# A fused attention and feed-forward kernel: TensorE kept in written order while the position bias is made, and one pair's operand splits moved from GpSimd to ScalarE and VectorE

## The chip, the cores and the metric

The kernel runs on one core of a Trainium2 chip. The metric is device time in microseconds (us) of one execution. One execution was also profiled; times inside it are counted from the start of its span. Engines are named as in the profile: PE is TensorE, with its weight loads as PEld; DVE is VectorE; ACT is ScalarE; POOL is GpSimd; SP only issues transfers. An "issue" row of SP (SPq) is the time that SP needs to hand a transfer over, not the transfer itself.

## The reference, cut to what matters

```python
scores = scale * np.matmul(q, k.transpose(0, 1, 3, 2))      # 4 batches, 8 heads, 576 x 576, head size 64
x = (np.log1p(abs(pos_i - pos_j)) / np.log1p(max(pos_i, 1)))[..., None]
bias = np.maximum(x @ w1 + b1, 0.0) @ w2                    # hidden size 32, one bias plane for each head
attn = softmax(scores + bias)                               # over the last axis
x = heads_side_by_side(attn @ v)                            # 4 x 576 x 512
u = x + np.real(fft(fft(x, axis=1), axis=2))
un = (u - mean(u)) / np.sqrt(var(u) + 1e-06)
out = u + np.maximum(un @ w_ch1, 0.0) @ w_ch2               # 512 -> 2048 -> 512
```

## The kernel before

The work falls into three stages.

**The bias stage** (some 80 us) makes the bias planes. It runs over 144 steps, four to a group `u` (36 groups). For each step one tile of hidden values is made: three of every four on VectorE (`hd`, L334, 108 in all) and one on ScalarE (`ha`, L332, 36). Two small matmuls of TensorE (L353) then reduce it into a PSUM tile `bps` of the group; there are three such tiles. ScalarE evacuates each group into one of four quarters of `ring` (L302, 36 evacuations), and after every fourth group SP sends that quarter out: to the `bias` tiles of head pair 0 in SBUF (L311, for the last groups `bias_r` in L218 to L221) and to DRAM (`bias_d`, L314). VectorE has eight buffers for `hd`, ScalarE six for `ha`.

**Attention** runs over 16 units, a unit being a pair of heads and a batch. A unit's q and k arrive by four transfers into `qT` and `kT` (one buffer each, so the next unit's loads wait until these are read). `prep` turns them into a rounded high part and a low rest, in eight splits: `qs` and `kh` by `hi` (L181), the low halves of `qs` and `kl` by `lo` (L184), all on GpSimd. There are two buffers of each. `scores` are four matmuls to a tile (L243), `largest` adds the bias and finds the row maximum on VectorE (L261, here called the maximum step), `expo` is the exponential on ScalarE (L269). Nine score tiles make a unit. Those of unit 0 are computed inside the bias stage already, by `first_scores`: tiles 0 to 5 in pairs at the steps that the list `due` names (a number WAIT after the step at which their bias rows begin a block), 6, 7 and 8 after its last step. During the bias stage there is one PSUM buffer for a score tile. Then come the turns, one for each unit; a turn's steps are written out in `ORDER`, and TensorE, VectorE and ScalarE keep that order. The steps `W0` to `W3` make one chunk of a weight matrix 32-bit: a transfer into `raw` (L138), one ScalarE instruction (L140, `wf`) and three of VectorE (L141 to L143). The first chunk's `raw` shares its buffer with `sm`, the small tables of the bias stage, so its transfer waits until that stage is over.

**The feed-forward stage** follows: the Fourier sums, the normalization and two matrix products.

What orders instructions: the compiler layer lists each engine's instructions by a simulated timeline, except on engines that a `manual_schedule` block keeps in written order. Before the change only the turns have such a block. Each engine then works through its own list in order and waits at an instruction whose inputs or buffers are not ready.

Of the kernel before, what the change touches and what calls it, by code (L numbers as in the profile page):

```python
# [9 lines left out]
F32 = mybir.dt.float32  # L10
# [3 lines left out]
AF = mybir.ActivationFunctionType  # L14
ALU = mybir.AluOpType
# [10 lines left out]
ND = 258  # L26
NF = FF // P
FCN = 15
L0, L1 = 0, 42
WAIT = 20  # L30
EV = 40
AHEAD = 19
HB = {"d": 8, "a": 6}
# [14 lines left out]
ORDER = """  # L48
# [61 lines left out]
def body(ctx, tc, a, out):  # L110
    nc = tc.nc
# [46 lines left out]
    def load(n):  # L158
        hp, b = units[n]
        t = []  # L160
        for nm, w in (("qT", 2 * S), ("kT", KW)):
            f = ldp.tile([P, w], F32, tag=nm, name=nm)
            for e in range(2):
                nc.sync.dma_start(f[64 * e:64 * e + 64], a[nm][hp, b])
            t.append(f)
        ld[n] = t

    def load_v(n):
        hp, b = units[n]
        v = vt[n] = vp.tile([P, 5, P], F32, tag="v", name="v")  # L170
        nc.sync.dma_start(v, a["v"][hp, b].rearrange("(t p) c -> p t c", p=P))

    def prep(n):
        q, k = ld.pop(n)
        qs = stp.tile([P, 2 * S], F32R, tag="qs", name="qs")
        kh = stp.tile([P, KW], F32R, tag="kh", name="kh")
        kl = stp.tile([P, KW], F32R, tag="kl", name="kl")
        stk[n] = (qs, kh, kl)

        def hi(dst, src, c):  # L180
            nc.gpsimd.tensor_scalar(dst[:, c], src[:, c], 1.0, 0.0, ALU.mult, ALU.add)  # L181

        def lo(dst, src, ref, rows, c):
            nc.gpsimd.tensor_tensor(dst[rows, c], src[rows, c], ref[rows, c].bitcast(F32), ALU.subtract)  # L184

        every, low = slice(0, 128), slice(64, 128)
        ca, cb, ck = slice(0, S), slice(S, 2 * S), slice(S, KW)
        return [
            lambda: hi(qs, q, ca), lambda: lo(qs, q, qs, low, ca),
            lambda: hi(kh, k, ca), lambda: lo(kl, k, kh, every, ca),  # L190
            lambda: hi(qs, q, cb), lambda: lo(qs, q, qs, low, cb),
            lambda: hi(kh, k, ck), lambda: lo(kl, k, kh, every, ck),
        ]
# [72 lines left out]
    def expo(n, i):  # L266
        blk = (BLK if n else BLK0)[i]
        p = prob(n, blk)
        nc.scalar.activation(  # L269
            p, p, AF.Exp, bias=nms[n][:, blk:blk + 1], scale=-1.0, accum_out=sums[n][:, blk:blk + 1])  # L270

    def first_scores(i):
        scores(0, i)
        largest(0, i)
        expo(0, i)

    with ExitStack() as st:
        hpool = pool("hp", 1, stack=st)
        ring = xp.tile([P, 4, 4, S], F32, tag="x", name="ring")
        bps = pool("bps", 3, PSUM, stack=st)  # L280
        sps = pool("sps0", 1, PSUM, stack=st)

        sm = rawp.tile([P, 66 + 5 * NG], F32, tag="raw", name="sm")
        w1c, b1c, w2 = sm[:, 0:1], sm[:, 1:2], sm[:, 2:66].rearrange("p (r c) -> p r c", r=2)
        lt, inv = sm[:, 66:66 + 4 * NG], sm[:, 66 + 4 * NG:]
        nc.sync.dma_start(sm, a["sm"])
        parts = ((512, 1148), (0, 512), (1148, NT0 + S))
        for i, (c0, c1) in enumerate(parts):
            (nc.sync if i else nc.scalar).dma_start(tw[:, c0:c1], a["tab"][:, c0:c1])
        nc.vector.tensor_scalar(lt, lt, b1c, None, ALU.mult)  # L290
        for i, (c0, c1) in enumerate(parts):
            if i == 9:
                nc.scalar.activation(tw[:, c0:c1], tw[:, c0:c1], AF.Copy, scale=w1c)
            else:
                nc.vector.tensor_scalar(tw[:, c0:c1], tw[:, c0:c1], w1c, None, ALU.mult)

        def bias_evac(u, ps):
            g = u % 4
            o = ring[:, u // 4 % 4]
            dst = o[:, g].rearrange("p (c s) -> p c s", c=2)  # L300
            if u % EV != EV - 1:
                nc.scalar.activation(dst, ps[:, :, :CH], AF.Copy, scale=inv[:, u:u + 1])  # L302
            else:
                nc.vector.tensor_scalar(dst, ps[:, :, :CH], inv[:, u:u + 1], None, ALU.mult)
            if g < 3:
                return
            r0 = 16 * (u - 3)
            src = o.rearrange("(r h) g s -> r h g s", h=H)
            for e in range(2):
                if r0 < 512:  # L310
                    nc.sync.dma_start(bt[0, r0 // 128][r0 % 128:r0 % 128 + 64, e], src[:, e])  # L311
                else:
                    rest_bias(bt[0, 4], e, src[:, e])
            nc.sync.dma_start(bias_d[4 * (u - 3):4 * (u + 1)].rearrange("r h g s -> (r h) g s"), o)  # L314
            if u % 8 == 7:
                due.extend([(4 * u + WAIT, u // 8 * 2), (4 * u + WAIT + 2, u // 8 * 2 + 1)])

        pending, early = [], []
        due = []
        ps = None  # L320
        steps = bias_steps()
        ahead = {}

        def hidden(n):
            u, t4, _, low, _ = steps[n]
            col = lt[:, 4 * u + t4:4 * u + t4 + 1]
            off = NT0 if low is None else N0 - low
            src = tw[:, off:off + S]
            who = WHO[n % len(WHO)]
            h = hpool.tile([P, S], F32, tag="h" + who, name="h" + who, bufs=HB[who])  # L330
            if who == "a":
                nc.scalar.activation(h, src, AF.Relu, bias=col)  # L332
            else:
                nc.vector.tensor_scalar(h, src, col, 0.0, ALU.add, ALU.max)  # L334
            return h

        for n, (u, t4, rev, low, _) in enumerate(steps):
            for k in range(n, min(n + AHEAD, len(steps))):
                if k not in ahead and (k <= n + 2 or WHO[k % len(WHO)] != "d"):
                    ahead[k] = hidden(k)  # L340
            if n in (L0, L1):
                load(n // L1)
                load_v(n // L1)
                early.extend(prep(n // L1))
            if early and n % 2:
                early.pop(0)()
            while due and due[0][0] <= n:
                first_scores(due.pop(0)[1])
            h = ahead[n]
            if t4 == 0:  # L350
                ps = bps.tile([P, 2, 512], F32, tag="ps", name="bps")
            for c in range(2):
                nc.tensor.matmul(  # L353
                    ps[32 * t4:32 * t4 + 32, c, :CH], w2[:, int(rev)], h[:, c * CH:(c + 1) * CH],
                    start=True, stop=True, tile_position=(0, 32 * t4),
                )
            if t4 == 3:
                pending.append((u, ps))
            if t4 == 2 and len(pending) > 1:
                bias_evac(*pending.pop(0))  # L360
        for e in pending:
            bias_evac(*e)
        for i in [i for _, i in due] + [8]:
            first_scores(i)


    x = xp.tile([P, B, 5, DM], F32, tag="x", name="x")
    with mid, ExitStack() as st:
# [112 lines left out]
        def first_column():  # L481
# [20 lines left out]
            engines={mybir.EngineType.PE, mybir.EngineType.DVE, mybir.EngineType.Activation}))  # L502
        for n in range(U + 4):
            pr = prep(n + 1) if 1 < n + 1 < U else []
            wd = []
            if n < NF:
                wf = rawp.tile([P, 512], F32, tag="wf", name="wf")
                wd = widen(a["m1"][:, P * n:P * n + P].rearrange("(k p) c -> p k c", p=P), wf, [P, 4, P], rawp)
            for i, w in enumerate(ORDER):
                w, u = w.rstrip("'"), n - w.count("'")  # L510
                if w[0] == "W":
                    if u < NF:
                        wd[int(w[1])]()
                elif 0 <= u < U and (u or w[0] not in "SDX"):
                    steps[w[0]](u, w)
                if i % 8 == 4 and pr:
                    pr.pop(0)()
            assert not pr
            if n < NF:
                nc.sync.dma_start(w1_d[n].rearrange("p k c -> p (k c)"), wf)  # L520
            if n + 2 < U:
                load(n + 2)
            if n == 6:
                fs = tabp.tile([P, 3, 2, 2, NK], F32R, tag="tab", name="fs")
                nc.gpsimd.tensor_copy(fs[0:1, 0, 0, 0, 0:1], vt[6][0:1, 0, 0:1])
                nc.gpsimd.dma_start(fs, a["fs"])
            if n == FCN:
                first_column()


    with ExitStack() as st:
# [201 lines left out]
        for b in range(B):  # L733
# [4 lines left out]
            if b + 1 < B:  # L738
                tl, un, pcs = prepare(b + 1)
                n = 4  # L740
            else:
                un, pcs = norm(rest_tiles)
                n = 2
# [67 lines left out]
```

## Time and profile before

| | |
|---|---|
| time, median of 3 runs | 814.06 us (811.08, 814.06 and one far longer, 4077.4) |
| time of the profiled execution | 811.41 us |
| its span, first to last instruction | 809.6 us |
| mean granted clock of TensorE, of full speed | 0.971 |
| PE busy | 762.1 us, 94% |
| DVE busy | 430.8 us, 53% |
| ACT busy | 432.1 us, 53% |
| POOL busy | 378.3 us, 47% |

The shares are means over stages that have different limits. The bias stage lies at 4 to 78 us of the span, the first turns run until about 100, the steady turns until about 320.

### The profile page before, as it was taken

To read this page: it belongs to the slowest core of one execution; us is meant where nothing else is said; L and a number is where in the kernel's file an instruction comes from. 1 tells how busy PE (TensorE), PEld (TensorE's weight loads), DVE (VectorE), ACT (ScalarE), POOL (GpSimd) and SP (SyncE) were. 2 spreads that over 40 slices of the span, in tenths; PEclk is the share of its full clock that TensorE was granted. 3 is DMA by queue.
4 is the path that set the end of the run, shared out by engine and by line. 5 is a ranking of instruction groups with operands and counts; after the bars stand their busy time and mean duration, and the time that the engine had idled before them with its cause. 6 is when DMAs were issued, how large, how long until landed. Compare 5 with 4: busy or idle time off the path is not lost. (4 is left out here: it accounts for less than half of the span.)

```text
span 809.6 us, 13075 instructions
## 1 busy us (share of the span) xinstructions
PE 762.1 (94%) x4786; PEld 619.8 (77%) x4786; DVE 430.8 (53%) x935; ACT 432.1 (53%) x875; POOL 378.3 (47%) x317
## 2 busy tenths in 40 slices
PE   3997799999999999957998999999999999999997
PEld 2454688878887888637886888888888887888896
DVE  5796666666666666889598351531417322111311
ACT  5696587787878787634433342333333333332453
POOL 5602364566446640032555534544346444444695
PEclk8899799999999999987999999999999999999999
DMA  6888568778747631174423221111210112111332
GB/s 158 249 261 303 151 170 261 211 182 250 199 119 206 189 96 41 66 259 157 140 95 117 92 91 39 40 53 51 80 53 27 55 49 91 53 45 47 118 91 66
DMA packets 55376, 101.63 MB, mean 126 GB/s; under 512 B 7568, under 2 KB 26128, under 8 KB 53904
## 3 DMA queue, kind: packets, MB, share of 16 engines
q1 hardware_dynamic: 54880, 97.44, 40.6%
q0 software_dynamic: 288, 3.02, 1.2%
q8 instruction: 38, 0.62, 0.3%
q10 hardware_dynamic: 144, 0.33, 0.1%
q14 instruction: 26, 0.21, 0.1%
HBM read 74.38 MB, written 23.72 MB: 121 GB/s over the span
## 5 line engine op out<-in xcount | busy, mean ns | idle before, releaser
L691 DVE SCALAR_TENSOR_TENSOR hl<-hp,hh 128x512 fp32r<-128x512 f32 (+1 forms) x80 | 50.7, 634 | 222.0 <-ACT hh L690 222.0
L663 POOL TENSOR_TENSOR w2l<-w2f,w2h 128x512 fp32r<-128x512 f32 x80 | 104.1, 1302 | 113.4 <-ACT w2h L662 108.4
L663 POOL TENSOR_TENSOR w1l<-w,w1h 128x512 fp32r<-128x512 f32 x80 | 108.2, 1353 | 93.4 <-ACT w1h L662 89.9
L261 DVE CUSTOM_DVE_ANT_0 p<-s,bias 128x576 f32<-128x576 f32 x128 | 95.5, 755 | 77.9 <-PE s L243 74.4
L685 PE MATMUL hp<-ul,w1h 128*128 128x512 f32 (+1 forms) x320 | 118.1, 369 | 1.4 <-DVE ul L655 1.4
L685 PE MATMUL hp<-uh,w1l 128*128 128x512 f32 (+1 forms) x320 | 118.0, 369 | 0.0
L685 PE MATMUL hp<-uh,w1h 128*128 128x512 f32 (+1 forms) x320 | 118.0, 369 | 0.0
L243 PE MATMUL s<-kh,qs 128*128 128x288 f32 (+1 forms) x320 | 101.2, 335 | 13.5 <-DVE nm L261 6.8
L699 PE MATMUL acc<-w2h,hh 128*128 128x512 f32 x288 | 112.2, 391 | 0.0
L699 PE MATMUL acc<-w2l,hh 128*128 128x512 f32 x288 | 112.0, 390 | 0.0
L662 ACT ACTIVATE w2h<-w2f 128x512 fp32r<-128x512 f32 x80 | 50.5, 632 | 114.6 <-POOL w1l L663 61.2
L381 ACT ACTIVATE pt<-t 128x512 f32<-128x512 f32 x144 | 82.5, 595 | 51.6 <-PE t L401 35.6
L699 PE MATMUL acc<-w2h,hl 128*128 128x512 f32 x288 | 105.3, 395 | 2.9 <-DVE hl L691 2.9
L662 ACT ACTIVATE w1h<-w 128x512 fp32r<-128x512 f32 x80 | 50.3, 630 | 105.0 <-PE hp L685 96.8
L269 ACT ACTIVATE p<-p,nm 128x576 f32<-128x576 f32 x128 | 98.0, 773 | 1.2 <-DVE nm L261 1.2
L181 POOL TENSOR_SCALAR kh<-kT 128x576 fp32r<-128x576 f32 (+1 forms) x32 | 28.8, 916 | 138.3 <-PE s L243 95.9
L243 PE MATMUL s<-kl,qs 128*128 128x288 f32 (+1 forms) x320 | 89.8, 298 | 0.0
L422 PE MATMUL o<-pt,v 128*64 128x288 f32 x640 | 86.7, 417 | 0.0
L243 PEld LDWEIGHTS s<-kh,qs 128*128 128x128 f32 (+1 forms) x320 | 59.3, 185 | 30.7 <-POOL kh L181 7.2
L401 PE MATMUL t<-ident,p 128*128 128x128 f32 x576 | 79.8, 275 | 0.3 <-ACT pt L381 0.3
L685 PEld LDWEIGHTS hp<-ul,w1h 128*128 128x128 f32 x320 | 60.4, 189 | 12.0 <-DVE ul L655 1.7
L401 PEld LDWEIGHTS t<-ident,p 128*128 128x128 f32 x576 | 68.4, 141 | 1.1 <-ACT pt L381 0.7
(125 smaller groups left out, 1377.4 us busy)
## 6 DMA issues: line engine op xcount, KB each, us to landing
raw<-m SPq DMA_DIRECT2D x32, 512.0 KB, 3.9
w2f<-w_d SPq DMA_DIRECT2D x64, 256.0 KB, 2.6
bias_d<-ring SPq DMA_DIRECT2D x9, 1152.0 KB, 6.1
kT<-kT SPq DMA_DIRECT2D x32, 304.0 KB, 5.0
qT<-qT SPq DMA_DIRECT2D x32, 288.0 KB, 4.5
bias<-bias_d SPq DMA_DIRECT2D x24, 288.0 KB, 5.0
v<-v SPq DMA_DIRECT2D x16, 320.0 KB, 3.2
out<-x SPq DMA_DIRECT2D x18, 256.0 KB, 2.7
```

What stands on the lines that cost most here:

```text
L181: nc.gpsimd.tensor_scalar(dst[:, c], src[:, c], 1.0, 0.0, ALU.mult, ALU.add)
L243: nc.tensor.matmul(ps[:m, c, :CH], qs[:, c0:c0 + m], kk[:, k0 + c * CH:k0 + (c + 1) * CH], start=k == 0, stop=k == 1, skip_group_check=True)
L261: nc.vector.tensor_tensor_reduce(p, bank.pop((n, i))[:, :, :CH], bias, -0.125, 3.0e38, ALU.add, ALU.min, nms[n][:, blk:blk + 1])
L269: nc.scalar.activation(p, p, AF.Exp, bias=nms[n][:, blk:blk + 1], scale=-1.0, accum_out=sums[n][:, blk:blk + 1])
L381: nc.scalar.activation(dst, src, AF.Copy)
L401: nc.tensor.transpose(tp[:, 128 * t:128 * t + 128], pb[t].rearrange("p h s -> p (h s)")[:, k0:k0 + 128], ident)
L422: nc.tensor.matmul(os_[u][e, c, :CH], vt[u][:, j, e], pts[u][:, 2 * j + h if j < 4 else 8, c * CH:(c + 1) * CH], start=j == 0, stop=j == 4 ...
L662: nc.scalar.activation(h, src, AF.Copy)
L663: nc.gpsimd.tensor_tensor(l, src, h.bitcast(F32), ALU.subtract)
L685: nc.tensor.matmul(ps[:, :N], (wh, wl)[wi][:, P * kb:P * kb + P], ut[ui][:, kb, :N], start=i == 0, stop=i == len(mm) - 1)
L691: nc.vector.scalar_tensor_tensor(hl[:, :N], ps[:, :N], 0.0, hh[:, :N].bitcast(F32), ALU.max, ALU.subtract)
L699: nc.tensor.matmul(acc[t], h[i][:, P * t:P * t + P], w[j], start=f == 0 and k == 0, stop=f == NF - 1 and k == 2)
```

## The change

In the bias stage TensorE is put in written order. With it the loads and the splits of unit 0 are written ahead of the loop. WAIT goes from 20 to 24. The eight splits of unit 1 are taken out of the loop and off GpSimd: `hi` becomes a copying ACTIVATE of ScalarE, `lo` a TENSOR_TENSOR of VectorE, and they are written between the score tiles 7 and 8 of unit 0, in a block in which TensorE, VectorE and ScalarE all keep the written order. In turn 0, `ORDER` is sorted so that the `W` steps come last.

```diff
-L0, L1 = 0, 42
-WAIT = 20
+L1 = 42
+WAIT = 24
...
         def hi(dst, src, c):
-            nc.gpsimd.tensor_scalar(dst[:, c], src[:, c], 1.0, 0.0, ALU.mult, ALU.add)
+            if n == 1:
+                nc.scalar.activation(dst[:, c], src[:, c], AF.Copy)
+            else:
+                nc.gpsimd.tensor_scalar(dst[:, c], src[:, c], 1.0, 0.0, ALU.mult, ALU.add)
 
         def lo(dst, src, ref, rows, c):
-            nc.gpsimd.tensor_tensor(dst[rows, c], src[rows, c], ref[rows, c].bitcast(F32), ALU.subtract)
+            eng = nc.vector if n == 1 else nc.gpsimd
+            eng.tensor_tensor(dst[rows, c], src[rows, c], ref[rows, c].bitcast(F32), ALU.subtract)
...
-        pending, early = [], []
+        pending = []
...
+        fixed = ExitStack()
+        fixed.enter_context(tc.manual_schedule(engines={mybir.EngineType.PE}))
+        load(0)
+        load_v(0)
+        early = prep(0)
         for n, (u, t4, rev, low, _) in enumerate(steps):
...
-            if n in (L0, L1):
-                load(n // L1)
-                load_v(n // L1)
-                early.extend(prep(n // L1))
+            if n == L1:
+                load(1)
+                load_v(1)
...
-        for i in [i for _, i in due] + [8]:
+        fixed.close()
+        fixed.enter_context(tc.manual_schedule(engines={
+            mybir.EngineType.PE, mybir.EngineType.DVE, mybir.EngineType.Activation}))
+        for _, i in due:
             first_scores(i)
+        for piece in prep(1):
+            piece()
+        first_scores(8)
+        fixed.close()
...
-            for i, w in enumerate(ORDER):
+            for i, w in enumerate(ORDER if n else sorted(ORDER, key=lambda w: w[0] == "W")):
```

**Where the first score tile stands on PE.** TensorE's list near the start of the bias stage; `bps` rows are the bias matmuls, `s` rows those of a score tile. Before:

```order
L353 MATMUL bps<-ha,sm 32x288 x2
L353 MATMUL bps<-hd,sm 32x288 x4
L243 MATMUL s<-kh,qs 128x288
L353 MATMUL bps<-hd,sm 32x288 x2
L353 MATMUL bps<-ha,sm 32x288 x2
L353 MATMUL bps<-hd,sm 32x288 x6
L353 MATMUL bps<-ha,sm 32x288 x2
L243 MATMUL s<-kl,qs 128x288
L243 MATMUL s<-kh,qs 128x288
L243 MATMUL s<-kl,qs 128x288
```

TensorE's list now, at the place of its first score tile:

```order
L361 MATMUL bps<-ha,sm 32x288 x2
L247 MATMUL s<-kh,qs 128x288
L247 MATMUL s<-kl,qs 128x288
L247 MATMUL s<-kh,qs 128x288
L247 MATMUL s<-kl,qs 128x288
L361 MATMUL bps<-hd,sm 32x288 x4
L247 MATMUL s<-kh,qs 128x288
L247 MATMUL s<-kl,qs 128x288
L247 MATMUL s<-kh,qs 128x288
L247 MATMUL s<-kl,qs 128x288
```

The first matmul on unit 0's splits stood after 18 steps (four groups and two steps); it now stands after 52 (13 groups), and the second tile of the pair only two steps behind the first.

**The first pair on DVE.** VectorE's list from there; the rows `p,nm` and `nm` are a maximum step. Before:

```order
L334 TENSOR_SCALAR hd<-tw,sm 128x576 x36
L261 ISA p,nm<-s,bias 128x576
L261 ISA nm 128x1
L334 TENSOR_SCALAR hd<-tw,sm 128x576 x8
L261 ISA p,nm<-s,bias 128x576
```

VectorE's list now, at the same place:

```order
L338 TENSOR_SCALAR hd<-tw,sm 128x576 x39
L265 ISA p,nm<-s,bias 128x576
L265 ISA nm 128x1
L338 TENSOR_SCALAR hd<-tw,sm 128x576 x2
L265 ISA p,nm<-s,bias 128x576
```

The first maximum step stands behind 47 hidden tiles (2, 6 and 39) where it stood behind 44, and two tiles part it from the second, where eight did. The later pairs move likewise.

**The end of the bias stage.** ScalarE's list; `p,sm` rows are exponentials, `ring` rows evacuations. Before:

```order
L302 ACTIVATE ring<-bps,sm 128x576 x2
L269 ACTIVATE p,sm<-p,nm 128x576
L302 ACTIVATE ring<-bps,sm 128x576 x5
L269 ACTIVATE p,sm<-p,nm 128x576 x2
L269 ACTIVATE pr,sm<-pr,nm 128x576
L140 ACTIVATE wf<-raw 128x512
```

ScalarE's list now, at the end of the stage:

```order
L306 ACTIVATE ring<-bps,sm 128x576 x5
L273 ACTIVATE p,sm<-p,nm 128x576
L306 ACTIVATE ring<-bps,sm 128x576
L273 ACTIVATE p,sm<-p,nm 128x576
L182 ACTIVATE qs<-qT 128x576
L182 ACTIVATE kh<-kT 128x576
L182 ACTIVATE qs<-qT 128x576
L182 ACTIVATE kh<-kT 128x640
L273 ACTIVATE pr,sm<-pr,nm 128x576
L140 ACTIVATE wf<-raw 128x512
```

The four `hi` splits stand ahead of tile 8's exponential, and the last evacuation (group 35) now stands behind tile 6's exponential. On VectorE the four `lo` splits stand likewise between the maximum steps of tiles 7 and 8. On SP, the four loads of unit 2, which stood among the bias transfers, now stand right behind the transfer of the first `raw`. No row of the first weight chunk (L140 to L143) has moved against its neighbours.

## Rows read from the trace of the kernel before

**Rows 1.** Windows: from:to, length, busy time (instructions) of each engine, PEclk, DMA share, GB/s.

```profile
13.50:20.00 6.50, 0.09 (x2) 0.00 (x0) 1.98 (x5) 1.45 (x3) 6.33 (x5) 0.69 0.05 12
39.80:72.00 32.20, 32.13 (x378) 19.06 (x372) 31.68 (x77) 30.66 (x53) 0.00 (x0) 1.00 0.83 271
100.00:120.00 20.00, 20.00 (x160) 16.00 (x157) 11.60 (x35) 17.11 (x41) 13.10 (x12) 1.00 0.60 168
```

**Rows 2.** Timeline of PE: start, length, engine, line, operation [idle before it <-what ended that].

```profile
20.30 0.61 PE L243 MATMUL s<-kh,qs 128*128 128x288 f32 x1 [6.71 <-POOL kh L181]
...
87.48 0.58 PE L243 MATMUL s<-kh,qs 128*128 128x288 f32 x1 [5.26 <-DVE nm L261]
...
102.30 0.40 PE L243 MATMUL s<-kh,qs 128*128 128x288 f32 x1
```

**Rows 3.** Timeline of DVE, the bias stage and the first turn.

```profile
9.38 6.10 DVE L334 TENSOR_SCALAR hd<-tw,sm 128x576 f32<-128x576 f32 x14
23.01 2.82 DVE L334 TENSOR_SCALAR hd<-tw,sm 128x576 f32<-128x576 f32 x4 [7.53 <-PE bps L353]
27.19 12.74 DVE L334 TENSOR_SCALAR hd<-tw,sm 128x576 f32<-128x576 f32 x18 [1.37 <-PE bps L353]
...
66.68 4.80 DVE L334 TENSOR_SCALAR hd<-tw,sm 128x576 f32<-128x576 f32 x11
73.09 0.76 DVE L261 CUSTOM_DVE_ANT_0 p<-s,bias 128x576 f32<-128x576 f32 x1 [1.61 <-DMA bias<-ring]
...
77.95 0.76 DVE L261 CUSTOM_DVE_ANT_0 pr<-s,bias_r 128x576 f32<-128x576 f32 x1 [2.43 <-DMA bias_r<-ring]
...
84.16 1.77 DVE L142 SCALAR_TENSOR_TENSOR raw<-raw 128x512 int32<-128x512 int32 x1
```

**Rows 4.** Timeline of POOL and DVE at single splits.

```profile
9.16 6.85 POOL L181 TENSOR_SCALAR qs<-qT 128x576 fp32r<-128x576 f32 x1 [7.86 <-DMA qT<-qT]
...
31.39 0.51 DVE L334 TENSOR_SCALAR hd<-tw,sm 128x576 f32<-128x576 f32 x1
...
31.51 0.92 POOL L181 TENSOR_SCALAR kh<-kT 128x576 fp32r<-128x576 f32 x1 [2.07 <-DMA kT<-kT]
...
33.56 1.65 DVE L334 TENSOR_SCALAR hd<-tw,sm 128x576 f32<-128x576 f32 x1
...
82.44 2.94 POOL L184 TENSOR_TENSOR qs<-qT,qs 64x576 fp32r<-64x576 f32 x2
```

**Rows 5.** Groups of POOL by shape at 27 to 40 us | busy, mean ns | idle.

```profile
L184 POOL TENSOR_TENSOR qs<-qT,qs 64x576 fp32r<-64x576 f32 x2 | 3.0, 1529 | 0.1
L184 POOL TENSOR_TENSOR kl<-kT,kh 128x640 fp32r<-128x640 f32 x1 | 1.8, 1752 | 0.0
L184 POOL TENSOR_TENSOR kl<-kT,kh 128x576 fp32r<-128x576 f32 x1 | 1.6, 1599 | 0.0
L181 POOL TENSOR_SCALAR kh<-kT 128x576 fp32r<-128x576 f32 x1 | 0.9, 919 | 2.1 <-DMA kT<-kT 2.1
```

**Rows 6.** Timeline of ACT, the bias stage and the first turn.

```profile
10.35 0.72 ACT L302 ACTIVATE ring<-bps,sm 128x576 f32<-128x576 f32 x1
...
11.64 0.72 ACT L302 ACTIVATE ring<-bps,sm 128x576 f32<-128x576 f32 x1
...
68.19 0.79 ACT L302 ACTIVATE ring<-bps,sm 128x576 f32<-128x576 f32 x1
...
72.77 0.74 ACT L302 ACTIVATE ring<-bps,sm 128x576 f32<-128x576 f32 x1 [0.55 <-PE bps L353]
73.89 0.78 ACT L269 ACTIVATE p<-p,nm 128x576 f32<-128x576 f32 x1 [0.39 <-DVE nm L261]
...
82.94 0.66 ACT L140 ACTIVATE wf<-raw 128x512 f32<-128x512 f32 x1 [3.32 <-DMA raw<-m]
```

**Rows 7.** Timeline of SP: the issue of the first weight chunk's transfer.

```profile
76.51 0.39 SPq L138 DMA_DIRECT2D raw<-m  x1
```

**Rows 8.** Groups of DVE by shape at 86 to 97 us.

```profile
L142 DVE SCALAR_TENSOR_TENSOR raw<-raw 128x512 int32<-128x512 int32 x1 | 0.7, 687 | 0.0
```

## The prediction

> **What bounds the kernel now.** I read the windows first [rows 1]. From 100 us on PE is busy all the time, so whatever the bias stage and the first turn gain or lose arrives at the end. Inside the stage it is different. At 13.5 to 20 us PE does nothing, and the PE timeline says why [rows 2]: the first score matmul waits 6.71 us for unit 0's `kh` from POOL, and all bias matmuls queue behind it. DVE then runs out of buffers and idles 7.53 us [rows 3]. At 27 to 40 us DVE never idles, yet 18 hidden tiles take 12.74 us, 0.71 each, where 14 tiles took 6.10 at 9.38, 0.43 from start to start. POOL, splitting unit 1 there, is the difference: single splits and hidden tiles stretch each other, a tile to 1.65 [rows 4, 5]. From 39.8 to 72 POOL is still, DVE and ACT are busy 31.7 and 30.7 of 32.2 us [rows 1], and PE follows them. So DVE and ACT set the stage, at 3 x 0.43 = 1.29 us a group on DVE and 1.29 on ACT (from evacuation to evacuation with one `ha` between, [rows 6]).
>
> At the end a chain of transfers takes over. Tile 6's maximum step waits for a bias transfer [rows 3]; the last evacuation ends at 73.51; SP issues the first weight chunk at 76.51 [rows 7]; it lands at 82.94 [rows 6]; L142 takes 1.77 us [rows 3]; and at 87.48 PE goes on, after 5.26 us of waiting for the maximum step behind the chunk [rows 2]. I take 87.48 as the mark: what it moves by, the kernel moves by.
>
> **PE in written order.** The stop at 13.6 us goes, since PE's first score tile now comes at step 52. What is late next? POOL still splits unit 0, now against a DVE that does not stop. Of the eight splits the first ends at 16.0. The other seven with DVE beside them have no row for unit 0; from below they cost DVE nothing, from above what the same seven shapes cost in unit 1 [rows 5]: 3 x 0.92 + 2 x 1.53 + 1.60 + 1.75 = 9.2 us. I take the upper, because these are the same instructions beside the same hidden tiles: POOL is done at 25.2. In unit 1's stretch DVE got one tile in for each split, so by 25.2 it has made its 22 tiles (of 15.4 us) and 8 more, 30. Alone it would have had 45.
>
> Step 52 needs 39 tiles: 25.2 + 9 x 0.43 = 29.1, and the splits that it reads were ready by about 23.5, so PE does not wait for POOL. The new wait is another one. DVE's first maximum step stands behind tile 47, at 29.1 + 8 x 0.43 = 32.5; until then PE holds at the pair's second score tile, which wants the only score buffer, with the bias matmuls behind it. ACT's first exponential, and the evacuations behind that, wait for it until 33.3. That is about 2.5 us of ACT idle, once: afterwards DVE is eight tiles ahead of PE and the later pairs find their maximum step at once, but for 0 to 0.35 us in each, in which DVE, after only two tiles (0.86), waits for the second score tile (an estimate: four matmuls of 0.40 [rows 2], started closely one behind the other, and two hand-overs, 0.9 to 1.2). I take 0.35.
>
> From 33.3 ACT has up to group 31: 17 pairs of 1.29, two evacuations of 0.72 and six exponentials of 0.78 [rows 6], 28.0 us, so group 31 leaves at 61.3 instead of 68.98, 7.7 earlier. From 32.5 DVE has 61 tiles of 0.43, six maximum steps of 0.76 and 3 x 0.35: 31.9, so its last tile is made at 64.4 instead of 71.48, 7.1 earlier. Both are near each other; I take **7.3**. Bounds: had POOL cost DVE nothing, ACT's own work from 10.35 on would bind (35 groups of 1.29, less 7 `ha` of 0.57 made early, six exponentials, 2.5 idle), about 12 earlier; with POOL held off altogether, the first rival below.
>
> **WAIT of 24** is part of that account: the bias rows of a pair are sent before step 4u + 4 of the next groups and landed some 4 us later, so no pair waits for them; 0.
>
> **Unit 1's splits.** Off POOL they free DVE at 27 to 40 us; that is in the 7.3. On ACT and DVE the trace shows no such split. The nearest rows are L140 on ACT, 0.66 at 512 columns, and the undisturbed L142 on DVE, 0.69 [rows 6, 8]: four of 576 to 640 columns make 3.1 us on each, 6.3 if they never overlapped. They stand behind tile 7's exponential, which ends about 3.2 us after tile 6's maximum step, and the chunk, which everything waits for next, is there 11.7 after it. So even 6.3 fits; I cost them at 0. They hold back tile 8's maximum step, which waited 2.43 us for its own transfer there anyway [rows 3]. Without that cover they would cost 3 to 6.
>
> **The last evacuation** now stands on ACT behind tile 6's exponential. That starts 0.80 after the maximum step [rows 3, 6], takes 0.7 to 0.8, and the evacuation 0.7: it ends 2.3 after tile 6's maximum step, where it ended 73.51 - 73.09 = 0.42 after it. SP's three `bias_r` transfers, `bias_d` and the chunk are queued behind it. **Loss 1.9**; at least 0, if the bias transfer lands earlier.
>
> **Unit 2's loads** wait for unit 1's `lo` splits, and SP issues them behind the chunk, 6 to 8 us after tile 6's maximum step; POOL therefore no longer works on unit 2 while L142 runs. Before, two splits at 82.44 did [rows 4], and L142 took 1.77 instead of 0.69 [rows 3, 8]. **Gain 1.1**, or 0 if they land together.
>
> The Trainium skill has a rule for these overlaps (SBUF — State Buffer, "Who interferes with whom"): a VectorE instruction in a two-port mode, or with two SBUF inputs, and a GpSimd instruction shut each other out for a whole instruction. The trace agrees, with 1.65 us beside 0.51 for a hidden tile [rows 4].
>
> **Turn 0 sorted** changes nothing: with n = 0 only the W steps are active, as all others carry a prime or are scores of unit 0, and the lists show no such row moved. In the feed-forward stage a few rows of PE and DVE swap places with neighbours, each of the size of L142; 0, with 1 us either way.
>
> **Sum:** -7.3 + 1.9 - 1.1 = -6.5. The mark goes from 87.48 to 81.0, and the time from the profiled execution's 811.41 to **804.9 us**. That execution lies 2.65 under the median of the three runs, 814.06, and beside the 811.08; I stay with its own time.
>
> **Rivals.** *POOL is held off* (15%). The first split took 6.85 us [rows 4] and ended half a microsecond after DVE's run of tiles did at 15.48: DVE may have kept POOL out as long as it ran without a pause. Then, with DVE no longer stopping at 15.4, POOL starts only when DVE sticks at the first maximum step: its tiles 23 to 47 end at 15.4 + 25 x 0.43 = 26.2, the seven splits that tile 0 needs take 0.6 + 2 x 0.67 + 2 x 1.4 + 1.4 + 0.7, about 6.9 (the last row's two `lo` take 2.94, so about 1.4 alone; 0.92 less the wait for a tile gives 0.67), tile 0's matmuls at half clock 1.2 and the step 0.76: 35.0 instead of 33.3, and the eighth split 1 more. Against it: the split at 31.51 got in after a single tile of a run as dense [rows 4]. Gain 4: 807.5. The Trainium skill's rule above, read as a lock that DVE never lets go, leads here. The Trainium skill also names another cause (GPSIMD Engine Reference, "Instruction dispatch"): the first call of freshly loaded code pays about 6 us. That fits 6.85 less a plain split, and by it the sum stays 804.9.
>
> *More is gained* (10%): DVE and POOL hinder each other less than in unit 1's stretch, and ACT's own work binds: 12 - 0.8 = 11.2 earlier, 800.2.
>
> *It is given back at the end* (12%): the splits are not covered because the chunk lands sooner, or the transfers crowd. 3 to 6 of the 6.5 go: 808 to 811.
>
> *Slower, by unit 2's operands* (4%). Its loads were done by 45 us; now the splits on POOL can begin only behind chunk and loads, at about 80 to 82, and take 8.5 us alone, 11 at the prices of rows 5. PE wants them at 102.30 - 6.5 = 95.8 [rows 2]. It decides from the point where they end later than that, and the kernel becomes slower than before from 102.3; at 105, 814. For it speaks that loads, weight chunk and `bias_r` share the transfers; against it the 4 us to spare.
>
> **How the numbers follow.** My forecast, 803 to 807, has 59%. For 8 in 10 the range takes in the larger gain and most of the given-back case: **800 to 810.5 us**. A measurement of this kernel can tell about 2% from no change, 16 us; ACT's own work in the stage keeps the gain under 12, so faster by over 2% gets 3%, slower 1%, within 2% 96%.
>
> **What would show it.** Right: no wait of PE at 13.6 us; hidden tiles of 0.9 to 1.7 us until about 25 and none later; one ACT idle of 2 to 3 us at about 30; tile 6's maximum step at 65.8; the last evacuation 2.3 after it; L142 at 0.7; the mark at 81. Wrong: a first split on POOL that ends at 26 (first rival), a wait of PE for POOL at unit 2's first score, or ACT or DVE at a split when `wf` has landed.

## The result, and the profile after

The changed kernel takes 820.57 us (median of 12 runs, 816.7 to 822.77), the kernel before 812.18 (median of 12 runs beside them, 808.24 to 814.9 but for one far longer). The ratio is **1.0099, 95% interval [1.0079, 1.0118]**: 8 us slower, where 804.9 and so a gain of some 7 was forecast. The profiled execution took 816.77 (span 815.0, granted clock 0.966). The two spans differ by only 5.4; the executions of either kernel spread over some 6 us, and the profiled one of before lies 3.2 over the lowest of its runs, this one 0.1. The mark (PE going on after the maximum step behind the first weight chunk) is at 95.64 instead of 87.48 [rows 2], 8.2 later, and the medians differ by 8.4. So by the mark the whole loss is there: 4.3 of the 8.2 at the first maximum step (44.13 instead of 39.85), 3.2 more at tile 6's (80.59 instead of 73.09), and 0.7 behind that. The first maximum step of the kernel before:

```profile
39.85 0.74 DVE L261 CUSTOM_DVE_ANT_0 p<-s,bias 128x576 f32<-128x576 f32 x1
```

Windows of the changed kernel (from:to, length, busy time and instructions of PE, PEld, DVE, ACT, POOL, then PEclk, DMA share, GB/s), to be read beside [rows 1]:

```profile
13.50:20.00 6.50, 6.43 (x82) 3.54 (x80) 6.50 (x16) 6.50 (x12) 6.50 (x1) 1.00 0.08 19
24.00:27.00 3.00, 0.00 (x0) 0.00 (x0) 2.12 (x5) 2.48 (x4) 3.00 (x2) 1.00 0.00 0
27.00:30.00 3.00, 0.00 (x0) 0.00 (x0) 0.00 (x0) 0.00 (x0) 2.92 (x3) 0.79 0.00 0
30.00:34.00 4.00, 1.62 (x4) 1.03 (x4) 0.00 (x0) 0.00 (x0) 3.91 (x5) 0.50 0.65 155
34.00:40.00 6.00, 2.15 (x9) 0.58 (x8) 0.00 (x0) 0.00 (x0) 0.43 (x1) 0.50 1.02 325
44.10:80.60 36.50, 33.55 (x384) 17.88 (x384) 31.33 (x74) 30.46 (x51) 0.00 (x0) 0.93 0.70 246
```

The hole at 13.5 to 20 us is closed: PE, DVE and ACT are full there. It has come back larger. From 27 to 34 only POOL works, but for four score matmuls of PE; from 34 to 40 DVE and ACT still do nothing, while the transfers run at full load and the granted clock is at its lower level of 1.2 GHz.

What POOL did until then (timeline: start, length, engine, line, operation, idle before; the first split by itself, the second left out):

```profile
9.75 16.90 POOL L184 TENSOR_SCALAR qs<-qT 128x576 fp32r<-128x576 f32 x1 [8.44 <-DMA qT<-qT]
...
27.38 2.75 POOL L188 TENSOR_TENSOR qs<-qT,qs 64x576 fp32r<-64x576 f32 x2
30.21 1.36 POOL L184 TENSOR_SCALAR kh<-kT 128x576 fp32r<-128x576 f32 x2
31.54 2.89 POOL L188 TENSOR_TENSOR kl<-kT,kh 128x576 fp32r<-128x576 f32 x2
```

And DVE beside it, up to the first maximum step, and at the end of the stage:

```profile
9.28 16.84 DVE L338 TENSOR_SCALAR hd<-tw,sm 128x576 f32<-128x576 f32 x39
44.13 0.76 DVE L265 CUSTOM_DVE_ANT_0 p<-s,bias 128x576 f32<-128x576 f32 x1 [18.01 <-DMA bias<-ring]
...
80.59 0.76 DVE L265 CUSTOM_DVE_ANT_0 p<-s,bias 128x576 f32<-128x576 f32 x1 [1.11 <-DMA bias<-ring]
...
93.50 0.69 DVE L142 SCALAR_TENSOR_TENSOR raw<-raw 128x512 int32<-128x512 int32 x1
```

39 hidden tiles in one group of 16.84 us, 0.43 from start to start: DVE never stopped and was never slowed. POOL's first split stands in the trace from 9.75 to 26.65, which ends 0.53 behind the last tile at 26.12: its 16.90 us are almost all waiting, since one of its size takes 0.67 alone. In [rows 4] the first split took 6.85 and ended as much behind a DVE run of 14 tiles [rows 3]. The other splits then ran alone, until 34.43.

PE waits for them, and then for DVE (its timeline; the third row is the second tile of the pair, the fourth the mark):

```profile
30.94 0.61 PE L247 MATMUL s<-kh,qs 128*128 128x288 f32 x1 [7.03 <-POOL kh L184]
32.99 0.61 PE L247 MATMUL s<-kl,qs 128*128 128x288 f32 x1 [1.44 <-POOL kl L188]
44.95 0.61 PE L247 MATMUL s<-kh,qs 128*128 128x288 f32 x1 [8.80 <-DVE nm L265]
...
95.64 0.61 PE L247 MATMUL s<-kh,qs 128*128 128x288 f32 x1 [2.84 <-DVE nm L265]
```

The score tile was there by about 34, but DVE's first maximum step came at 44.13, and what it waited for last was a bias transfer. SP's queue shows why (issues, in order):

```profile
30.15 1.11 SPq L164 DMA_DIRECT2D qT<-qT  x2
31.31 1.25 SPq L315 DMA_DIRECT2D bias<-ring  x2
32.60 0.59 SPq L318 DMA_DIRECT2D bias_d<-ring  x1
34.46 1.91 SPq L164 DMA_DIRECT2D kT<-kT  x2
36.48 1.75 SPq L315 DMA_DIRECT2D bias<-ring  x2
38.27 0.59 SPq L318 DMA_DIRECT2D bias_d<-ring  x1
```

SP hands transfers over one by one. Unit 1's `qT` must wait until POOL has read unit 0's, at 30.13, and the bias rows of the first groups, evacuated long before, stand behind it; then `kT` waits for the last split (34.43), with the next bias rows behind that.

At the end of the stage ACT shows the last evacuation where it was expected, behind tile 6's exponential, and the four `hi` splits behind tile 7's:

```profile
81.39 0.78 ACT L273 ACTIVATE p<-p,nm 128x576 f32<-128x576 f32 x1 [0.94 <-DVE nm L265]
...
82.16 0.72 ACT L306 ACTIVATE ring<-bps,sm 128x576 f32<-128x576 f32 x1
...
85.53 0.72 ACT L182 ACTIVATE kh<-kT 128x640 fp32r<-128x640 f32 x1
...
92.34 0.66 ACT L140 ACTIVATE wf<-raw 128x512 f32<-128x512 f32 x1 [3.06 <-DMA raw<-m]
```

### The profile page after: what moved, and what is told of

Same layout as the page of the kernel before. It is cut to its first block, busy times and chain, and to the rows that moved or that the text cites. A ratio compares the mean times of both kernels' runs of the same rounds, so it can differ in the third digit from the quotient of the medians.

```text
span 815.0 us, 13064 instructions
## 1 busy us (share of the span) xinstructions
PE 759.9 (93%) x4786; PEld 617.5 (76%) x4786; DVE 428.1 (53%) x939; ACT 433.8 (53%) x879; POOL 378.4 (46%) x309
## 5 line engine op out<-in xcount | busy, mean ns | idle before, releaser
L247 PE MATMUL s<-kh,qs 128*128 128x288 f32 (+1 forms) x320 | 103.4, 341 | 21.1 <-DVE nm L265 13.8
L247 PE MATMUL s<-kl,qs 128*128 128x288 f32 (+1 forms) x320 | 91.9, 304 | 1.6 <-POOL kl L188 1.4
L184 POOL TENSOR_SCALAR qs<-qT 128x576 fp32r<-128x576 f32 x30 | 36.2, 1224 | 73.6 <-DMA qT<-qT 70.9
```

The lines of the kernel that those rows point to most:

```text
L247: nc.tensor.matmul(ps[:m, c, :CH], qs[:, c0:c0 + m], kk[:, k0 + c * CH:k0 + (c + 1) * CH], start=k == 0, stop=k == 1, skip_group_check=True)
```

## The experiments

The theory after the result has two links. *Lock-out*: a run of hidden tiles without a gap keeps POOL (its first split, at least) out until DVE pauses. In the kernel before, TensorE's stop at 13.6 us made that pause; the written order took it away. *Queue*: unit 1's load, waiting for POOL's reads, holds up the bias transfers behind it. Rivals: only the first call on POOL is slow or kept out, and what follows alternates with DVE; the moved splits cost the time; the written order costs it by itself. The expectations call the lock-out theory 1 and the first of the rivals theory 2. All ratios are to the kernel before on the same chip; its medians on the other three chips were 811.43 (e1 to e4), 811.31 (e5 to e8) and 809.78 (e9 to e11). "Mark" is read as above (87.48 before, 95.64 after).

| kernel | first maximum step | tile 6's | mark | median | ratio, 95% interval |
|---|---|---|---|---|---|
| before | 39.85 | 73.09 | 87.48 | 812.18 | |
| changed | 44.13 | 80.59 | 95.64 | 820.57 | 1.0099 [1.0079, 1.0118] |
| e1_warm | 44.39 | 80.89 | 96.14 | 817.83 | 1.0091 [1.0059, 1.0123] |
| e9_full_warm | 44.25 | 80.92 | 96.38 | 817.02 | 1.0073 [1.0048, 1.0099] |
| e2_order_alone | 44.83 | 81.15 | 95.83 | 817.99 | 1.0074 [1.0044, 1.0104] |
| e3_splits_alone | 33.16 | 68.14 | 82.06 | 802.73 | 0.9879 [0.9842, 0.9917] |
| e5_load_late | 34.17 | 74.29 | 89.89 | 809.76 | 0.9980 [0.9960, 1.0001] |
| e6_one_pause | 32.98 | 68.02 | 83.06 | 807.59 | 0.9951 [0.9925, 0.9976] |
| e10_copy_no_wait | 32.49 | 67.48 | 82.48 | 807.57 | 0.9950 [0.9924, 0.9976] |
| e4_unit0_off_pool | 29.86 | 64.82 | 79.86 | 797.54 | 0.9812 [0.9768, 0.9857] |
| e7_evac_first | 29.96 | 64.89 | 79.92 | 805.80 | 0.9943 [0.9923, 0.9963] |
| e8_order_undone | 26.47 | 60.90 | 74.85 | 800.07 | 0.9873 [0.9836, 0.9909] |
| e11_wait20 | 28.14 | 64.33 | 79.60 | 802.34 | 0.9897 [0.9848, 0.9946] |

**Which part of the change costs?** Each half alone (there is no unit 99, so in the first every split stays on GpSimd, and unit 1's are started at step 42, with its load):

```diff
 e2_order_alone: changed kernel, unit 1's splits back in the loop on GpSimd
-            if n == 1:
+            if n == 99:
...
+                early.extend(prep(1))
...
-        for piece in prep(1):
-            piece()
 e3_splits_alone: changed kernel, TensorE scheduled as before
-WAIT = 24
+WAIT = 20
-        fixed.enter_context(tc.manual_schedule(engines={mybir.EngineType.PE}))
```

> The changed kernel with unit 1's eight splits left on GpSimd and in the loop from step 42, as before; TensorE's written order, WAIT of 24 and the sorted turn 0 stay. Theory 1 puts the loss on the written order, which takes away the pause in which GpSimd got its slot: the first split ends at about 26, the bias transfers stand behind unit 1's load, the first maximum step comes at about 44, and the time is at least that of the changed kernel, 1.010 to 1.015 of before. If instead the moved splits of unit 1 were what costs the time, this kernel comes to about before, 0.995 to 1.002.

> The changed kernel with TensorE scheduled as before in the bias loop and WAIT of 20; unit 1's splits stay on ScalarE and VectorE at the stage's end, with that block in written order. Theory 1: TensorE's first score matmul stays early, VectorE runs out of buffers at about 15.5 us and GpSimd gets in there, the first split takes 6 to 7 us; from 27 to 40 no split disturbs VectorE, whose 18 hidden tiles take 0.43 instead of 0.71, 5 us less; the end of the stage costs 1.9 and gives 1.1 back; tile 6's maximum step at about 68 to 69 instead of 73.1 and the time 0.994 to 0.998 of before. If the moved splits cost the time, it is slower than before, 1.005 to 1.010.

The written order alone brings the loss, with the stall in the same place:

```profile
44.83 0.76 DVE L265 CUSTOM_DVE_ANT_0 p<-s,bias 128x576 f32<-128x576 f32 x1 [18.14 <-DMA bias<-ring]
```

Its 1.0074 lies below the 1.010 to 1.015 that was expected, but its interval overlaps that of the changed kernel. The moved splits alone gain 1.2%; tile 6 is where it was expected (68.14), the time lower than that. There the first split took 6.86 us and ended 0.53 after DVE's fourteenth tile, as before. So the two halves are not a sum: the splits' gain (DVE undisturbed at 27 to 40) is gone once DVE stands still there anyway.

**Is it the first call on POOL?** Two kernels prepare POOL ahead of DVE's run, one with single columns, one with the full size of a split:

```diff
 e1_warm
+    warm = const.tile([P, 2], F32R, tag="warm", name="warm")
+    nc.gpsimd.tensor_scalar(warm[:, 0:1], ident[:, 0:1], 1.0, 0.0, ALU.mult, ALU.add)
+    nc.gpsimd.tensor_tensor(warm[:, 1:2], ident[:, 0:1], warm[:, 0:1].bitcast(F32), ALU.subtract)
 e9_full_warm
+    full = stp.tile([P, KW], F32R, tag="kh", name="full")
+    copy = stp.tile([P, KW], F32R, tag="kl", name="copy")
+    nc.gpsimd.memset(full.bitcast(F32), 1.0)
+    for _ in range(2):
+        nc.gpsimd.tensor_scalar(copy[:, :S], full[:, :S].bitcast(F32), 1.0, 0.0, ALU.mult, ALU.add)
```

> The changed kernel, with one TENSOR_SCALAR and one TENSOR_TENSOR of a single column on GpSimd ahead of everything, so that neither form is new to GpSimd when unit 0's first split comes. Theory 1 (VectorE's gapless run of hidden tiles keeps GpSimd out until VectorE pauses): the first split still ends about 26 us, half a microsecond behind VectorE's run; the first maximum step stays at about 44; the time is that of the changed kernel, 1.010 of before. Theory 2 (only the first call of each form is slow or held off, and warm splits alternate with hidden tiles): the first split ends by about 12, all eight by about 25, the first maximum step comes at 30 to 35, tile 6's at 66 to 72, and the time is 0.992 to 0.998 of before.

> The changed kernel, with a memset and two TENSOR_SCALARs of the full size of a split (128 x 576, same form) on GpSimd ahead of VectorE's run of hidden tiles. It asks whether the first full-size split of the program is kept out because it is the first, which the single columns could not show. If it is: the first real split gets in after a tile or two, the eight splits end by about 25, the first maximum step comes at 31 to 36 and the time is 0.990 to 0.997 of before. If what decides is only that VectorE's run has no pause when GpSimd asks: the split again ends half a microsecond behind VectorE's run at about 26.6, and the time is 1.007 to 1.012.

POOL's timeline in the second one:

```profile
2.31 1.42 POOL L203 TENSOR_SCALAR copy<-full 128x576 fp32r<-128x576 f32 x2
9.30 17.65 POOL L184 TENSOR_SCALAR qs<-qT 128x576 fp32r<-128x576 f32 x1 [5.58 <-DMA qT<-qT]
```

The same instruction that takes 0.7 us at 2.31, when DVE is not yet running, takes 17.65 beside DVE's run. In both kernels stall and time are those of the changed one: it is not that the call is the first.

**What opens the door?** One column copied on DVE, first so that it waits for POOL, then so that it waits for nothing:

```diff
 e6_one_pause
+            if n == 5:
+                gap = const.tile([P, 1], F32, tag="gap", name="gap")
+                nc.vector.tensor_copy(gap, stk[0][0][:, 0:1].bitcast(F32))
 e10_copy_no_wait
+            if n == 23:
+                gap = const.tile([P, 1], F32, tag="gap", name="gap")
+                nc.vector.tensor_copy(gap, ahead[20][:, 0:1])
```

> The changed kernel with one copy of a single column of qs on VectorE behind its 14th hidden tile, so that VectorE pauses there until GpSimd's first split is done. Both theories: the first split ends 0.5 to 0.7 after VectorE's last tile ahead of the copy, at about 15.5 to 16. Theory 1 in its strict form (every split of GpSimd needs a pause of VectorE): the second split is kept out from there to the end of VectorE's run at about 26.6, the other splits end at about 34, the first maximum step comes at about 43 and the time is 1.006 to 1.010 of before. Theory 2 (only the first split at the start of the program is kept out; after that VectorE and GpSimd alternate, as beside unit 1's splits in the kernel before): the eight splits end by about 25, hidden tiles of 0.9 to 1.7 stand among the others, the first maximum step comes at 31 to 36, and the time is 0.990 to 0.997 of before.

> The changed kernel with a copy of one column of an older hidden tile on VectorE in the middle of its run (behind the 17th hidden tile, at about 13 us), which waits for nothing of GpSimd. If any break in the row of hidden tiles lets GpSimd in: the first split ends 0.5 to 1 after the copy, at about 14, the rest alternates with hidden tiles, and the time is 0.990 to 0.997 of before, as with the copy that waited. If VectorE must stand idle: the first split ends at about 26.6 as in the changed kernel and the time is 1.007 to 1.012.

DVE with the copy that waits for nothing, tile by tile, and its tile 6:

```profile
12.75 0.52 DVE L338 TENSOR_SCALAR hd<-tw,sm 128x576 f32<-128x576 f32 x1
13.19 0.15 DVE L357 COPY gap<-hd 128x1 f32<-128x1 f32 x1
13.25 0.86 DVE L338 TENSOR_SCALAR hd<-tw,sm 128x576 f32<-128x576 f32 x1
...
32.49 0.75 DVE L265 CUSTOM_DVE_ANT_0 p<-s,bias 128x576 f32<-128x576 f32 x1
...
67.48 0.76 DVE L265 CUSTOM_DVE_ANT_0 p<-s,bias 128x576 f32<-128x576 f32 x1 [1.15 <-DMA bias<-ring]
```

and POOL beside it:

```profile
9.20 4.60 POOL L184 TENSOR_SCALAR qs<-qT 128x576 fp32r<-128x576 f32 x1 [7.88 <-DMA qT<-qT]
...
14.72 3.07 POOL L188 TENSOR_TENSOR qs<-qT,qs 64x576 fp32r<-64x576 f32 x2
17.88 1.65 POOL L184 TENSOR_SCALAR kh<-kT 128x576 fp32r<-128x576 f32 x2
```

The first split now ends at 13.80, 0.53 behind the tile ahead of the copy, and from there splits and tiles alternate one for one; the eight splits are done at 22.80. DVE did not stand idle for it: a 0.15 us copy of another kind of instruction in the row was enough, and against before the kernel is at 0.9950 instead of 1.0099. With the copy that waits, which the compiler layer put earlier than I had counted, DVE's run ended at 11.69, the first split at 12.22, and the picture is the same from there. So the strict form of the theory, that every split needs a pause, fell: only the first entry does, and a break in the row, of the one sort that was tried, will do for it.

**How much is the queue?** SP in written order in the loop, and unit 1's loads 30 steps later:

```diff
 e5_load_late
-L1 = 42
+L1 = 72
-        fixed.enter_context(tc.manual_schedule(engines={mybir.EngineType.PE}))
+        fixed.enter_context(tc.manual_schedule(engines={mybir.EngineType.PE, mybir.EngineType.SP}))
```

> The changed kernel with SP in written order too in the bias loop and unit 1's loads moved from step 42 to 72, so that the first bias transfers stand ahead of them on SP's queue; nothing about GpSimd changes. If the loss has two links (GpSimd kept out until VectorE pauses, and unit 1's load, waiting for GpSimd's reads, holding up the bias transfers behind it): GpSimd's first split still ends at about 26.6 and all eight at about 34.4, but the first bias transfers are issued at about 20 and VectorE's first maximum step waits only for the score tile: 33 to 36 instead of 44.1, tile 6's at 70 to 73 instead of 80.6, and the time falls to 0.994 to 1.000 of before. If the queue is no link of it, the first maximum step stays at about 44 and the time at 1.010. The other list that differs is ScalarE's, with the last evacuation ahead of tile 6's exponential, worth up to 1.9.

The lock-out is unchanged (POOL's last split ends at 34.49), the first bias rows go out at 15.17, and the first maximum step now waits for the score tile:

```profile
34.17 0.76 DVE L265 CUSTOM_DVE_ANT_0 p<-s,bias 128x576 f32<-128x576 f32 x1 [7.99 <-PE s L247]
```

ACT's first exponential follows:

```profile
34.98 0.78 ACT L273 ACTIVATE p<-p,nm 128x576 f32<-128x576 f32 x1 [8.19 <-DVE nm L265]
```

10 of the 18 us of DVE's wait were the queue, 8 the lock-out; in time, 1.2% came back. Tile 6 came 1 to 4 us later than expected: the second tile of the pair and the bias matmuls ran at a granted clock of 0.59 at 34 to 40, and the moved loads stood on SP's queue at 46 to 51, ahead of the next bias rows, for which the third pair then waited 2.21. How much each cost was not separated.

**POOL out of the stage, and then the order by itself.**

```diff
 e4_unit0_off_pool: changed kernel
-            if n == 1:
+            if n <= 1:
-            eng = nc.vector if n == 1 else nc.gpsimd
+            eng = nc.vector if n <= 1 else nc.gpsimd
 e8_order_undone: the same, and
-WAIT = 24
+WAIT = 20
-        fixed.enter_context(tc.manual_schedule(engines={mybir.EngineType.PE}))
 e11_wait20: e4, and
-WAIT = 24
+WAIT = 20
```

> The changed kernel with unit 0's eight splits on ScalarE and VectorE too, so that GpSimd does nothing in the bias stage and unit 1's load has no GpSimd reader to wait for. Theory 1 (GpSimd kept out, and through it the load and the bias transfers queued behind it): VectorE's hidden tiles go on undisturbed, four splits longer; unit 1's load and the first bias transfers are issued about 20 us as before; the first maximum step at 32 to 35, tile 6's at 66 to 70, the mark at 81 to 85, the time 0.992 to 0.998 of before. If the 18 us of VectorE's wait come from TensorE's order itself or from the bias transfers, not from GpSimd, the first maximum step stays at about 44 and the time at about 1.010.

> The kernel with units 0 and 1 off GpSimd, but with TensorE scheduled as before in the bias loop and WAIT of 20. It asks what the written order is worth when GpSimd is out of the stage. Theory 1: the operands are ready by about 17, so the early score matmul stops TensorE for 3 us at most; the first maximum step comes at 29 to 33 and the time is within 3 us of the kernel with the written order, 0.978 to 0.986 of before. If the written order by itself costs time, apart from GpSimd, this kernel is faster than that one by 3 us or more, 0.977 or less.

> The kernel with units 0 and 1 off GpSimd, in written order, but with WAIT back at 20. Its two neighbours differ by 5 us at the mark (79.0 in written order with 24, 74.0 in the scheduled order with 20). If WAIT is what costs, since it puts the first pair eight hidden tiles later on VectorE than ScalarE can use: the first maximum step comes at 26 to 28 and the mark at 75 to 77. If the written order itself costs, because TensorE stands at the second score tile of each pair with the bias matmuls behind it: the first maximum step comes earlier too, but each pair still costs ScalarE 1.5 to 2.5 us, and the mark stays at 78 to 80.

Without POOL there is no stall, and e4 is the fastest kernel of the study, 1.9% under before: everything in it came 1 to 2 us earlier, and its time 1% lower, than expected. Undoing the order (e8) brings the mark from 79.86 to 74.85, but no lower time: 0.9873, above the 0.978 to 0.986 that was expected, with an interval that meets e4's. With WAIT back at 20 and the written order kept (e11), the first maximum step comes 1.7 earlier than in e4 and the mark stays. The marks of e8 and e11, which differ in the order alone:

```profile
74.85 0.40 PE L247 MATMUL s<-kh,qs 128*128 128x288 f32 x1 [1.73 <-DVE nm L265]
...
79.60 0.61 PE L247 MATMUL s<-kh,qs 128*128 128x288 f32 x1 [2.99 <-DVE nm L265]
```

So the 4.8 us are the written order's own; 3.4 of them are there at tile 6's maximum step (60.90 in e8, 64.33 in e11). (The 79.0 and 74.0 in the expectation are the start of the maximum step behind the chunk, 0.8 ahead of the mark.) ACT shows them at the first pair of e11:

```profile
28.93 0.78 ACT L273 ACTIVATE p<-p,nm 128x576 f32<-128x576 f32 x1 [1.25 <-DVE nm L265]
...
30.99 0.78 ACT L336 ACTIVATE ha<-tw,sm 128x576 f32<-128x576 f32 x1 [1.20 <-PE bps L361]
```

1.25 and 1.20 of idle time, as in e4 (1.21 and 1.19). In the scheduled order the only idle time of ACT there is this:

```profile
29.64 0.78 ACT L336 ACTIVATE ha<-tw,sm 128x576 f32<-128x576 f32 x1 [0.36 <-PE bps L360]
```

In time the 4.8 us hardly show: e8 has 0.9873 and e11 0.9897, with overlapping intervals. Where e4 makes them good after the mark was not tested. In the feed-forward stage e8's and e11's instructions stand in the same order, and e4's in another, so the times of e4 and e8 compare more than the bias stage.

**The last evacuation.** In e4, the last evacuations put into the block that all three engines keep in order:

```diff
 e7_evac_first
-        for e in pending:
-            bias_evac(*e)
         fixed.close()
         fixed.enter_context(tc.manual_schedule(engines={
             mybir.EngineType.PE, mybir.EngineType.DVE, mybir.EngineType.Activation}))
+        for e in pending:
+            bias_evac(*e)
```

> The kernel with units 0 and 1 off GpSimd, and the last evacuations of the bias stage written into the block that all three engines keep in order, so that the last one stands ahead of tile 6's exponential. If my term of 1.9 for the last evacuation holds, it ends about 0.4 after tile 6's maximum step instead of 2.3, the mark comes 1.9 earlier, and the time is 1.9 lower than with the splits alone off GpSimd, about 795.6 (0.979 of before). If something else sets the chunk's transfer (the bias transfers ahead of it on SP), the mark and the time stay.

The evacuation ended 1.3 earlier and SP issued the chunk at 68.45 instead of 69.69, but it was used no sooner (first row: e7):

```profile
76.62 0.66 ACT L140 ACTIVATE wf<-raw 128x512 f32<-128x512 f32 x1 [3.02 <-DMA raw<-m]
```

In e4 the same instruction starts at 76.56. The mark does not move. In e7 the chunk's first packet moved at 72.59, 4.1 us after the issue, behind the transfers ahead of it, and from 66 us on the DMA share is 0.94 or more. Nine tenths of the packets had landed at 74.20 (75.32 in e4), but the last only at 75.58 (75.70 in e4), and the chunk is used when it is whole. Why the last ones were late stays open. The kernel as a whole is 1.3% slower than e4, with the mark in the same place: its lists also differ from e4's in the feed-forward stage, where TensorE's rows of the Fourier sums and of the matrix products stand in another order, as in e8 and e11. That difference was not meant, and what it costs was not measured by itself. It may be part of e4's 1.9%: e7, without POOL in the bias stage too, is only 0.6% under before.

## Why the prediction was wrong

**The step that failed** is "PE in written order": "I take the upper, because these are the same instructions beside the same hidden tiles: POOL is done at 25.2". That took the alternation of [rows 5] for a law, from the start of the run. But in [rows 5] POOL had already been let in once. Where it first asks beside a run it is not, and [rows 4] showed it: 6.85 us for a split of 0.67, ended half a microsecond behind DVE's run. The forecast counted that as the past ("the first ends at 16.0") and not as an effect of the stop that the change removes. Here POOL was done at 34.43. e10 shows that this step was the main fault: let in by one copy, POOL was done at 22.80 and the first maximum step came at 32.49 (forecast 32.5), tile 6's at 67.48 (65.8), the mark at 82.48 (81.0), and the time was 0.9950 of before (0.992).

**The first rival** had the mechanism, and its sum of 35.0 for ACT's start is what e5 measured (34.17 for the maximum step, 34.98 for the exponential). It was given 15% on the strength of the split at 31.51, which came after the first entry, and its time of 807.5 lacked the second link: nowhere did the text ask what SP has queued behind a load that waits for POOL. That queue made 8 us of wait into 18. With both links the first rival meant a loss, and not its gain of 4. Even without the queue the gain was less: e5 is at 0.9980, some 2 us.

**The 7.3 of the stage** was also 1.7 too high where POOL is let in (32.49 to 67.48 is 35.0, not 33.3): the later pairs were costed too low. The first pair cost ACT in e10 what was forecast, some 2.5 us (1.36 ahead of its exponential and 1.19 ahead of the next `ha`); at the second and third it waited 0.76 and 0.80 more, where 0.35 of DVE had been put for each pair, 1.05 in all, and DVE waited 2.5. The waits of e10 at 30 to 70 us (total, times, longest):

```profile
ACT ha L336 <- PE bps L364: 2.7, 3, 1.2
DVE hd L338 <- PE bps L364: 2.5, 6, 0.7
```

ACT's waits at the three pairs add up to 4.1; in e11 they are 4.0 where e8 has 0.4, which is the written order's price again.

**The bound of "about 12 earlier"** does not follow from its terms: 10.35 + 45.15 - 3.99 + 4.68 + 2.5 is 58.7 for the start of the last evacuation, 14 earlier than 72.77 [rows 6]. The rival with the larger gain (800.2) and the cap on the gain rest on it; neither was reached here.

**WAIT of 24 at 0** was right in size: in e4's kernel 20 instead moves the mark by 0.3. But its reason, that no pair waits for its bias rows, failed in the changed kernel with the queue: the first pair waited 18.01 for them. **Unit 1's splits at 0** were right in kind: the last `lo` split ended at 87.71 and the chunk was used at 92.34; tile 8's maximum step followed the splits at once. **L142** took 0.69 as forecast (the 1.1). **The last evacuation** ended 2.29 after tile 6's maximum step, forecast 2.3; the mark came 15.05 after it, forecast 15.2. The chunk was used 11.75 after that step, forecast 11.7, but in e7, with the last evacuation early, 11.73: the sum was right, but by luck as far as e7 shows, and what cost the 1.9 stays open. **Unit 2's operands** decided nothing: POOL began them at 95.09, when their `qT` had landed, still ahead of the turn that reads them. What the mark moved by (8.2), the time moved by (8.4): that step held in the changed kernel, but not in all the others: the median of e4 fell by 6 us more than its mark (its feed-forward stage is ordered otherwise, see above), and that of e5 by 4 more.

The Trainium skill (SBUF — State Buffer, "Who interferes with whom") says of these overlaps that whoever issues first gets the shared pair for the whole instruction and the other blocks. The runs agree on the block but not on its length: in the changed kernel POOL was kept out to the end of a run of 39 instructions, not of one. Its other rule that I weighed (GPSIMD Engine Reference, "Instruction dispatch", some 6 us for the first call of freshly loaded code) is not what held the split: the 17.65 us in e9 came behind two calls of the same form.

## What to carry to other kernels

A long wait that ended just when another engine paused is a dependence on that pause: before removing a stop, ask who got in through it. A helper engine's first work beside a dense run of VectorE may need a place made for it: here a one-column copy in the row gave it (e10), and moving the work to engines with room made it needless (e4). And when a consumer becomes late, look at what the in-order transfer queue holds behind the load that waits for it.

## What the runs showed of the hardware

- A run of VectorE TENSOR_SCALARs, 0.43 us from start to start with each one 0.51 long, so that each begins before the last has ended, kept a GpSimd TENSOR_SCALAR of the same size, the first split beside it, out until its end: 6.85, 16.90 and 17.65 us for one of 0.67. The split ended 0.53 behind the last tile each time.
- A single COPY of 128 x 1 in that run let GpSimd in, with VectorE never idle; after that the two alternated. In the kernel before, too, the split at 31.51 got in after one tile, though POOL had been still for 2.07 us [rows 4]. Why the first entry differs from the later ones stays open: the hidden tiles ahead of it and behind it look alike in the trace.
- The price of a stop goes on after it: after 7.03 us without a matmul TensorE came back at the lower clock level (0.50 granted at 30 to 40 us), in which a score matmul took 0.61 us instead of 0.40.
